# A linear-attention and SoLU kernel: the order of its work rewritten behind the first third, with halved squares and a new last unit

## The chip, the core and the metric

The kernel runs on one NeuronCore of a Trainium2 chip. The core has a matrix engine (TensorE: PE, with its weight loads listed apart as PEld), a vector engine (VectorE: DVE), an activation engine (ScalarE: ACT), a general engine (GpSimd: POOL) and a queue engine that mostly issues DMA transfers (SyncE: SP). Each has its own in-order queue, and they meet by semaphores. The metric is the device time of one execution in microseconds.

## What is computed

The first part is a linear attention with a decaying state, over 4 batches, 8 heads, 768 steps and head dimension 48. The second is a feed-forward layer on its output, read as 3072 tokens of 384 numbers: SoLU (h times softmax of h), a layer norm without shift, and the output product.

```python
for t in range(S):
    cur = einsum('bhd,bhe->bhde', u * k[t], v[t])
    y[t] = einsum('bhd,bhde->bhe', r[t], state + cur)
    state = w[t][..., None] * state + einsum('bhd,bhe->bhde', k[t], v[t])
h = x @ w_in                                   # 384 -> 1024
solu = h * softmax(h)
out = ((solu - mean) / sqrt(var + 1e-6) * g_ln) @ w_out   # 1024 -> 384
```

## The kernel before

The 768 steps are cut into six chunks of 128, and each chunk of each batch is a unit: unit i is chunk i // 4 of batch i % 4, 24 units in all. Inside a unit the recurrence is written as matrix products, and the state goes from unit i to unit i + 4.

One unit passes through these steps, each named by a word:

- LW, LK, LR, LV load the four inputs. The letter behind the point is the queue: none for SP, a for ACT, g for POOL.
- lw (ACT) takes the logarithm of the decays, cum (PE) sums it by two triangular matrices, ex (ACT) takes the exponentials in PSUM, and kp (DVE) multiplies keys and receptances by them.
- krk and krr (PE) turn these to the layout that the scores need and kr copies them from PSUM (ACT or DVE). In later units one DMA transpose, kt, takes the place of all three. It is issued by SP and reads and writes SBUF.
- M (PE) makes eight score blocks. m copies them out under the causal mask on DVE, or on ACT with the mask put on by POOL (sel).
- p, q (POOL), dg (DVE) and dv (POOL) make the diagonal term from r, k, u and v; vb casts v to bf16 on ACT or POOL.
- Y (PE) adds state and score products into y. Mode n leaves the diagonal term to y.d (DVE adds it while it copies y out); mode i adds it on PE by one more product of 384 columns with the identity, and then y.a copies on ACT.
- S (PE) makes the new state's sum, et (ACT) its decay, st (DVE) the decayed state. In mode n of S the old state is not added by PE: a DVE sum into the fp32 tile `sn_t` in SBUF goes ahead of the product. The old order uses this mode nowhere.
- X (three PE transposes) and xT (a copy) turn y for the next product; a DMA transpose on SP, xt, is the other way.
- H (24 matmuls of 128 columns) makes the hidden layer by columns, e (ACT) the exponential, he (DVE) their product, hq (ACT) the scaled square. For units named by an ht word the hidden layer is made by rows: six matmuls of 512 columns, and the statistics come from ACT's accumulators; a DMA transpose (ht) then turns he. The old order does this for units 16, 18 and 20.
- ea (POOL) adds the two halves of e, so that PE needs four sums of e in place of eight. The function `square_add` with its word qa does the same for the squares, in place; the old order has no qa word.
- Oa and Ob (PE) make the output's halves: per block of 128 hidden numbers one product of 386 columns and the sums over e and over the squares, one or two columns wide, in the same PSUM tile.
- qm (DVE), lv and rs (ACT) turn the sums into a scale, o scales the output (ACT or DVE) and out stores it from SP.

The last unit's hidden layer goes in halves (HA, HB, EA, EB, DA, DB, QA, QB). PSUM has eight banks, and the digit in a word says from which one it writes; a bank is free again when its last reader is done.

All this is written out by hand in one string, `ORDER`, of 881 words. The program runs through it and issues each word's instructions on its engine, so the string fixes the order on every queue. No planner moves anything afterwards. Rings of buffers bound how far a word may run ahead: 7 for inputs, 10 for lw and vb, 6 for kp, kr and dv, 4 for most others, 3 for p and q.

Almost every instruction is recorded under line 86 of the program, in the class `InOrder` that issues them, so the profile is read by tile names: `ps` is PSUM, `win_f` holds the row-wise he of the units named by ht, and `out<-in` names what is written and read.

Of the kernel before, what the change touches and what calls it, by code (L numbers as in the profile page):

```python
# [8 lines left out]
F32 = mybir.dt.float32  # L9
# [5 lines left out]
COPY = mybir.ActivationFunctionType.Copy  # L15
# [5 lines left out]
ORDER = """  # L21
# [11 lines left out]
Y5.n5 kp10 LR11 y5.d p8 LK11.a LK13 LW15 Ob1 X4.5 ex8 M7.1 lv0 krk10.4 rs0 kp8 q6 o0.a LK9.a vb6.p LW12 LR9 qm1  # L33
krr10 hq3.a dg6 cum11.6 q8 m7.d xT4.a Oa3.5 LV9.a lv1 out0 rs1 o1.a kr10.d out1 vb7.p vb8.a q7 ex11 LR12.g S7.0
LK12.a dv6 hq2.a LR14.g dg7 H4.2 et7 LK15.g lw9 e4 dg8 lw12 Ob3 kp11 st7 dv7 p10 krk8.1 qm3 cum9.6 Oa2.4 ex9 lv3
he4 Y7.n0 krr8 rs3 LW14.a o3.a Y6.n2 hq4.a kp9 y7.d LR17.g S6.3 Ob2 y6.d kr8.d p9 LW17 et6 X5.7 st6 LW19 qm2
LV12.a X7.2 krk11.6 vb9.a krr11 LR13 cum12.0 krk9.5 out3 xT7.d krr9 LK17 LK14 xT5.a lw15 lv2 kr11.d M8.2 q10 rs2
ex12 H5.6 o2.d q9 m8.a kp12 dv8 M11.3 lw13 S8.0 kr9.d m11.d p11 M9.1 LW16.a Oa4.5 e5 Ob4 m9.a et8 ea5.p he5
LR15.a X6.2 st8 vb11.p xT6.d sel8 out2 M10.3 p12 lw14 kt12 lw17 qm4 LV10 cum13.6 cum14.1 hot2.0 m10.d Y8.n0 S9.3
LR16.g hq5.a ex14 LW20 sel9 dg9 lv4 kp14 ex13 LW18.a Oa5.4 rs4 cum17.1 o4.a kp13 S11.5 y8.d et9 out4 cum15.6 Ob5  # L40
kt14 ex17 et11 ex15 Y9.n0 kp17 vb10.a H6.1 qm5 q11 dv9 lv5 rs5 LV15.g kp15 X8.6 st9 dg11 LR18.g y9.d LK16 o5.a
out5 lw19 dg10 e6 p13 kt15 H7.3 dv11 LV13 LW21.g xT8.a q12 he6 e7 vb12.p H8.6 hq6.a lw16 st11 he7 kt13 dg12
M12.1 X9.0 Oa6.5 p15 xT9.a dv10 Y11.n3 lw18 LK20.g m12.d Ob6 e8 p14 y11.d qm6 LV17 hq7.a he8 lv6 Y10.n2 LK18
M15.0 m15.d q13 rs6 y10.d dv12 q14 q15 H9.3 Oa7.7 Ob7 o6.a X10.0 LV14.a e9 LV16.g out6 hq8.a xT10.a he9 Y12.n5
p17 lw21 vb15.p vb14.p hq9.a xt11 qm7 y12.d M14.1 S10.3 Oa8.0 cum16.4 m14.d LK21.g et10 lv7 S12.1 st10 rs7
LK19.g LW22 dg15 dg13 Ob8 LR19.g vb13.a xt12 cum18.2 o7.a et12 ex16 H11.6 qm8 lv8 st12 kp16 out7 ex18 rs8 dv15
o8.a e11 dv13 S15.1 et15 dg14 H12.4 ea11.p e12 kp18 vb17.a q17 LR21 vb16.a out8 LV19.g LV21 lw22 he11 kt16
LV18.g hq11.a S13.3 p16 st15 Oa9.0 LR22.g Y15.n7 he12 LR20 y15.d Ob9 LK22 q16 M13.4 cum21.1 qm9 lv9 m13.d ex21
kp21 H10.6 p19 xt15 et13 rs9 Oa11.5 o9.a cum19.0 e10 Ob11 p18 st13 he10 qm11 hq12.a ex19 dg17 out9 Y13.n2 Oa12.4
Ob12 lv11 lw20 y13.d kt18 hq10.a rs11 dv14 vb19.p q18 M16.2 kt17 X13.7 kp19 Y14.n6 qm12 p21 vb18.a LK23 S16.0  # L50
xT13.a S14.7 lv12 rs12 o12.a m16.d y14.d cum20.1 et16 out12 et14 dg16 st14 q19 H13.3 H15.6 dg18 st16 ex20 xt14
o11.a Oa10.5 kp20 e13 dv16 M17.0 out11 ea13.p he13 dg19 cum22.2 e15 p20 ex22 dv17 Y16.i4 he15 Ob10 kp22 y16.a
H14.6 hq13.a e14 qm10 LW23.g q20 p22 M18.3 dv18 q22 ea15.p S18.2 LV20 lv10 kt19 m17.d Y17.n1 m18.d hq15.a Oa13.0
y17.d et18 dg20 st18 Ob13 rs10 he14 M19.3 ea14.p o10.a xt16 vb20.p qm13 H16.1 e16 kt22 dv20 Y18.n6 X17.5 m19.d
lv13 kt20 y18.d out10 xT17.a q21 rs13 Oa15.7 LV22.g Ob15 he16 M20.4 qm15 hq14.a S17.3 lv15 m20.d H17.1 dg21 et17
st17 kt21 M21.5 dv19 rs15 LR23 o15.a e17 m21.d Oa14.4 Ob14 he17 lw23 o13.a qm14 cum23.5 Y19.n3 xt18 Y20.n7 ex23
y19.d lv14 out15 y20.d ht16 LV23 ea17.p vb22.p rs14 vb21.a o14.a H18.0 p23 e18 X20.2 dg22 M22.3 S19.7 hq17.a
kp23 xT20.d m22.d Oa16.6 sv16 dv21 Y21.n5 hq16.a sv18 vb23.a Ob16 sq16 et19 H20.2 out13 he18 q23 y21.d dg23 dv22
e20 st19 xt19 he20 H19.0 Y22.n5 Oa17.7 kt23 e19 dv23 qm16 Ob17 y22.d ht18 M23.4 xt21 he19 lv16 rs16 o16.d Oa18.3
Ob18 hq20.a H21.0 hq18.a hq19.a m23.d ht20 xt22 out14 sq18 sv20 qm18 e21 lv18 ea19.p Y23.n2 rs18 Oa19.6 qm17  # L60
ea21.p lv17 rs17 y23.d Ob19 he21 Oa20.5 hq21.a qm19 out16 H22.0 o17.d xt23 lv19 o18.d rs19 Oa21.2 HA23.3 Ob21
out18 HB23.4 e22 Ob20 o19.d EA23 he22 hq22.a EB23 qm21 sq20 DA23 ea22.p lv21 qm20 lv20 DB23 QB23.d rs21 Oa22.7
# [38 lines left out]
def kernel(  # L101
# [14 lines left out]
    C = 128  # L116
# [462 lines left out]

    first_half, second_half = hidden_half(0), hidden_half(1)  # L580

    split = "out23.h" in ORDER.split()

    def output(i, part):
        L = live[i]
        e, he, hq, o_ps = e_t[i % NWK], he_t[i % NWK], hq_t[i % NWK], L["o_ps"]
        if i == NU - 1 and part and split:
            for f in range(KF // 2, KF):
                pe.matmul(o_ps[:, :DM + 2], lhsT=he[:, f, :], rhs=w2[:, f, :], start=False, stop=False,
                          skip_group_check=True)  # L590
            for f in range(KF // 2, KF):
                pe.matmul(o_ps[:, DM:DM + 2], lhsT=e[:, f, :], rhs=inv_col, start=False, stop=False,
                          skip_group_check=True)
            for f in range(KF // 2, KF):
                pe.matmul(o_ps[:, DM + 2:], lhsT=hq[:, f, :], rhs=one_col[:, :1], start=False, stop=(f == KF - 1),
                          skip_group_check=True)
            return
        for f in range(part * KF // 2, (part + 1) * KF // 2):
            if i in by_rows:
                pe.matmul(o_ps[:, :DM + 1], lhsT=he[:, f, :], rhs=w2[:, f, :DM + 1], start=(f == 0), stop=(f == KF - 1))  # L600
                continue
            pe.matmul(o_ps[:, :DM + 2], lhsT=he[:, f, :], rhs=w2[:, f, :], start=(f == 0), stop=False,
                      skip_group_check=True)
            if i not in added:
                pe.matmul(o_ps[:, DM:DM + 2], lhsT=e[:, f, :], rhs=inv_col, start=False, stop=False,
                          skip_group_check=True)
            elif f % 2 == 0:
                pe.matmul(o_ps[:, DM:DM + 2], lhsT=ea_t[i % NWK][:, f // 2, :], rhs=inv_col, start=False, stop=False,
                          skip_group_check=True)
# [37 lines left out]
    def scaled_out(i, x):  # L647
        o_ps, rs, o = live[i]["o_ps"], rs_t[i % NWK], o_t[i % NWK]
        if i == NU - 1 and split:
            act.activation(out=o[:, :DM // 2], in_=o_ps[:, :DM // 2], func=COPY, scale=rs)  # L650
            dve.tensor_scalar(out=o[:, DM // 2:], in0=o_ps[:, DM // 2:DM], scalar1=rs, scalar2=None, op0=MULT)
            return
        if x == "d":
            dve.tensor_scalar(out=o, in0=o_ps[:, :DM], scalar1=rs, scalar2=None, op0=MULT)
        else:
            act.activation(out=o, in_=o_ps[:, :DM], func=COPY, scale=rs)

    def store(i, x):
        c, b = units[i]
        rows = out[b * S + c * C:b * S + (c + 1) * C, :]  # L660
        if x == "h":
            act.dma_start(out=rows[:, :DM // 2], in_=o_t[i % NWK][:, :DM // 2])
            sp.dma_start(out=rows[:, DM // 2:], in_=o_t[i % NWK][:, DM // 2:])
            return
        queue[x].dma_start(out=rows, in_=o_t[i % NWK])

# [47 lines left out]
```

## Time and profile before

| | |
|---|---|
| time, median of 3 runs | 143.78 us (143.21 to 145.59) |
| the profiled execution's own time | 142.83 us |
| its span, first to last instruction | 141.0 us |
| PE busy | 125.5 us (89%) |
| DVE busy | 122.3 us (87%) |
| ACT busy | 118.9 us (84%) |
| POOL busy | 118.3 us (84%) |
| granted TensorE clock, mean | 0.99 |

The busy times are of one execution. Busy shares are averages over stages with different limits, so the stretches of the span have to be read apart. PE's matmuls are pipelined and their ends are modelled: a matmul's duration reaches beyond the start of the next one, and the time that one costs is the step from start to start.

### The profile page before, as it was taken

The page shows a single profiled execution, that of the slowest core. Times are in us where ns is not written, and L with a number is a line of the kernel's source. Part 1 is how long each engine was busy: PE and PEld are TensorE (multiplying, and loading weights), DVE is VectorE, ACT ScalarE, POOL GpSimd, SP SyncE. Part 2 cuts the span into 40 slices and gives each one's busy share as a digit, 9 for nine tenths or more (in the row PEclk, how much of TensorE's full clock was granted, in tenths as well). Part 3 has the DMA queues.
Part 4 walks back from the last instruction along what each step waited for, and adds up shares of the span by engine and source line. Part 5 has one row for each costly group of instructions (what it writes and reads, how often), then busy time and mean ns, then how long its engine had stood idle before and what let it go on. Part 6 is the DMA issues. An engine that isn't in the chain of part 4 may idle for free.

```text
span 141.0 us, 4797 instructions
## 1 busy us (share of the span) xinstructions
PE 125.5 (89%) x1890; PEld 94.6 (67%) x1890; DVE 122.3 (87%) x202; ACT 118.9 (84%) x243; POOL 118.3 (84%) x152
## 2 busy tenths in 40 slices
PE   0597956978999999999999999999999999999960
PEld 0136535657967887669877788788867766788740
DVE  6048879997999999999999998999999999878750
ACT  3648799979999999999989979998767889897780
POOL 7999999989999999999999999999999984402300
PEclk9999999999999999999999999999999999999996
DMA  4999999999999999999999999999999499652324
GB/s 89 274 298 343 323 278 388 382 307 232 263 234 237 285 297 295 242 227 223 297 190 238 188 242 213 291 224 162 186 228 213 97 255 86 144 170 78 123 73 154
DMA packets 94569, 31.98 MB, mean 227 GB/s; under 512 B 88569, under 2 KB 92674, under 8 KB 94546
## 3 DMA queue, kind: packets, MB, share of 16 engines
q1 hardware_dynamic: 70578, 20.92, 69.9%
q10 hardware_dynamic: 21984, 4.65, 15.6%
q0 software_dynamic: 1984, 6.10, 14.5%
q8 instruction: 15, 0.25, 0.8%
q14 instruction: 8, 0.07, 0.2%
HBM read 22.03 MB, written 4.72 MB: 190 GB/s over the span
## 4 chain that ended last, share of the span: by engine, by line
PE 40%; POOL 15%; DMA 13%; DVE 8%; ACT 5%; issue 2%; SPq 0%; ACTq 0%; POOLq 0%
PE ps L86 40%; DMA win_f<-in_moe_w_in_dram 5%; DMA kr_in<-in_k_dram 5%; DMA xT<-y 3%; POOL w L86 3%; POOL q L86 3%; DVE m L86 2%; POOL dv L86 2%; DVE he L86 2%; POOL m L86 2%; DVE y L86 1%; POOL win_sb L86 1%; ACT ps L86 1%; DVE kp L86 1%; POOL v_in L86 1%
## 5 line engine op out<-in xcount | busy, mean ns | idle before, releaser
L86 PE MATMUL ps<-w,he 128*128 128x386 bf16 (+1 forms) x192 | 43.2, 324 | 0.0
L86 PE MATMUL ps<-xT,win_sb 128*128 128x128 bf16 x504 | 31.2, 219 | 0.4 <-DMA xT<-y 0.2
L86 PEld LDWEIGHTS <-win_sb 128*128 128x128 bf16 x504 | 29.0, 98 | 2.1 <-DMA xT<-y 0.4
L86 ACT ACTIVATE e<-ps 128x1024 bf16<-128x1024 f32 (+1 forms) x25 | 24.6, 986 | 6.6 <-PE ps L86 5.0
L86 DVE TENSOR_TENSOR kp<-ps,kr_in 128x768 bf16<-128x768 f32 x24 | 22.7, 951 | 7.4 <-DMA kr_in<-in_r_dram 3.8
L86 PE MATMUL ps<-one_col,hq 128*128 128x1 bf16 x168 | 27.4, 163 | 0.0
L86 DVE TENSOR_TENSOR he<-ps,e 128x1024 bf16<-128x1024 f32 (+1 forms) x22 | 25.6, 1170 | 1.6 <-ACT e L86 1.3
L86 DVE TENSOR_TENSOR m<-ps,keep 128x1024 bf16<-128x1024 f32 x22 | 26.6, 1216 | 0.4 <-PE ps L86 0.4
L86 POOL TENSOR_TENSOR p<-kr_in 128x384 bf16<-128x384 f32 x24 | 24.0, 1004 | 0.3
L86 ACT ACTIVATE hq<-he 128x1024 bf16<-128x1024 bf16 (+1 forms) x21 | 21.6, 1030 | 0.7 <-DVE he L86 0.7
L86 POOL TENSOR_TENSOR q<-p,u_bc 128x384 bf16<-128x384 bf16 x24 | 21.7, 914 | 0.1
L86 POOL TENSOR_TENSOR dv<-vb,dg 128x384 bf16<-128x384 bf16 x24 | 19.8, 831 | 2.1 <-DVE dg L86 1.9
L86 ACT ACTIVATE ps<-ps 128x768 f32<-128x768 f32 x24 | 18.9, 796 | 2.6 <-PE ps L86 2.4
L86 PEld LDWEIGHTS <-he 128*128 128x128 bf16 x192 | 18.1, 96 | 3.5
L86 PEld LDWEIGHTS <-hq 128*128 128x128 bf16 x168 | 14.5, 96 | 8.8
L86 POOL TENSOR_TENSOR ea<-e 128x512 bf16<-128x512 bf16 x9 | 10.3, 1151 | 8.3 <-ACT e L86 8.3
L86 ACT ACTIVATE lw<-w_in 128x384 bf16<-128x384 f32 x24 | 12.3, 520 | 4.9 <-DMA w_in<-in_w_dram 4.9
L86 PE MATMUL ps<-inv_col,e 128*128 128x2 bf16 x96 | 15.8, 165 | 0.0
L86 PEld LDWEIGHTS <-kp 128*128 128x128 bf16 x176 | 11.8, 102 | 3.6 <-DVE kp L86 1.9
L86 PEld LDWEIGHTS <-kr 64*128 64x128 bf16 (+1 forms) x272 | 10.2, 95 | 5.3 <-issue 1.9
L86 DVE TENSOR_REDUCE dg<-q 128x8 f32<-128x384 bf16 x24 | 12.8, 544 | 0.2 <-POOL q L86 0.2
L86 DVE TENSOR_TENSOR st<-ps,et 128x384 bf16<-128x384 f32 x20 | 10.9, 549 | 0.6 <-ACT et L86 0.6
(97 smaller groups left out, 271.8 us busy)
## 6 DMA issues: line engine op xcount, KB each, us to landing
out_dram<-o SPq DMA_DIRECT2D x24, 192.0 KB, 3.7
kr_in<-in_k_dram SPq DMA_DIRECT2D x13, 192.0 KB, 5.8
kr_in<-in_r_dram POOLq DMA_DIRECT2D x12, 192.0 KB, 4.8
w_in<-in_w_dram SPq DMA_DIRECT2D x11, 192.0 KB, 5.2
kr_in<-in_r_dram SPq DMA_DIRECT2D x10, 192.0 KB, 4.8
v_in<-in_v_dram SPq DMA_DIRECT2D x10, 192.0 KB, 5.7
v_in<-in_v_dram POOLq DMA_DIRECT2D x9, 192.0 KB, 4.3
w_in<-in_w_dram ACTq DMA_DIRECT2D x8, 192.0 KB, 3.6
```

What stands on the lines that cost most here:

```text
L86: made = make(*args, **kwargs)
```

## The change

The first 250 words stay as they are. Behind them all words are in a new order, 633 of them in place of 631; queues, banks and modes change with them:

- x is turned by DMA in twelve units (8, 10, 11, 14, 15, 17 to 23) in place of ten (11, 12, 14, 15, 16, 18, 19, 21, 22, 23). Unit 14's keys and receptances are turned by PE, not by DMA.
- Unit 16 goes by columns like most others; only units 18 and 20 are left by rows.
- POOL halves the squares (qa) of units 12, 14, 15, 16, 17, 19 and 21, and the e of units 4, 7, 13, 16, 17, 19, 21 and 22 (before: 5, 11, 13, 14, 15, 17, 19, 21 and 22).
- S has mode n in units 12, 13, 14, 16 and 19. Y has mode i in units 8, 10, 11, 14 and 17 behind the cut, in place of unit 16.
- Two warm-up matmuls of 512 columns go. Several copies, casts and outputs change between ACT, DVE and POOL, and several loads change their queue: POOL issues one load more.
- The last unit's output has its first 256 columns in one bank, its sums of e and squares in a bank of their own, and the other 128 columns in a third. The sums are made ahead of most of the wide products. ACT scales and stores the 256 columns, DVE scales the 128 and SP stores them.

```diff
-    split = "out23.h" in ORDER.split()
+    ending = [word[2:].partition(".s") for word in ORDER.split() if word.startswith(f"Ob{NU - 1}.s")]
+    split = bool(ending)
+    DL = DM * 2 // 3
+
+    def last_output(i, part):
+        L = live[i]
+        e, he, hq = e_t[i % NWK], he_t[i % NWK], hq_t[i % NWK]
+        half = range(part * KF // 2, (part + 1) * KF // 2)
+        first = 2
+        if part == 0:
+            for f in range(first):
+                pe.matmul(L["o_ps"], lhsT=he[:, f, :], rhs=w2[:, f, :DL], start=(f == 0), stop=False)
+            L["s_ps"] = bank([C, 3], F32, ending[0][2][0], "s_ps")
+        s_ps = L["s_ps"]
+        for f in half:
+            pe.matmul(s_ps[:, :2], lhsT=he[:, f, :], rhs=w2[:, f, DM:], start=(f == 0), stop=False,
+                      skip_group_check=True)
+            pe.matmul(s_ps[:, :2], lhsT=e[:, f, :], rhs=inv_col, start=False, stop=False, skip_group_check=True)
+        for f in half:
+            pe.matmul(s_ps[:, 2:], lhsT=hq[:, f, :], rhs=one_col[:, :1], start=False, stop=(f == KF - 1),
+                      skip_group_check=True)
+        if part:
+            for f in range(first, KF):
+                pe.matmul(L["o_ps"], lhsT=he[:, f, :], rhs=w2[:, f, :DL], start=False, stop=(f == KF - 1))
+            r_ps = L["r_ps"] = bank([C, DM - DL], F32, ending[0][2][1], "r_ps")
+            for f in range(KF):
+                pe.matmul(r_ps, lhsT=he[:, f, :], rhs=w2[:, f, DL:DM], start=(f == 0), stop=(f == KF - 1))
...
-        o_ps = live[i]["o_ps"]
-        dve.tensor_scalar(out=qm_t[i % NWK], in0=o_ps[:, DM:DM + 1], scalar1=o_ps[:, DM + 1:DM + 2],
-                          scalar2=o_ps[:, DM + 2:], op0=MULT, op1=ADD)
+        s_ps = live[i]["s_ps"] if i == NU - 1 and split else live[i]["o_ps"][:, DM:]
+        dve.tensor_scalar(out=qm_t[i % NWK], in0=s_ps[:, :1], scalar1=s_ps[:, 1:2], scalar2=s_ps[:, 2:],
+                          op0=MULT, op1=ADD)
...
-            act.activation(out=o[:, :DM // 2], in_=o_ps[:, :DM // 2], func=COPY, scale=rs)
-            dve.tensor_scalar(out=o[:, DM // 2:], in0=o_ps[:, DM // 2:DM], scalar1=rs, scalar2=None, op0=MULT)
+            act.activation(out=o[:, :DL], in_=o_ps, func=COPY, scale=rs)
+            dve.tensor_scalar(out=o[:, DL:], in0=live[i]["r_ps"], scalar1=rs, scalar2=None, op0=MULT)
...
-QA23.a rs20 out17 Ob22 qm22 o20.a out19 lv22 Oa23.6 o21.d rs22 Ob23 out20 out21 o22.a qm23 lv23 rs23 out22 o23.a
-out23
+hq22.a lv20 rs20 EB23 DA23 Oa22.2 o20.d Ob22 QA23.a lv21 DB23 qm22 Oa23.0 QB23.d lv22 rs22 rs21 Ob23.s43 o22.a
+o21.a qm23 lv23 out20 rs23 out22 out21 o23.a out23.h
```

The last lines are the ends of the old and the new order.

More of the change, by code (lines that the diff above doesn't have):

```diff
@@ L37 @@
[L37 to L61, printed above, removed]
@@ new lines @@
+lv2 rs2 lw12 out0 LW16.a out1 LW14.g dv6 o2.a st6 S7.2 kr8.d et7 Ob3 LR17.g krk11.0 kp9 X5.1 M8.3 krr11 xT5.a
+st7 krk9.7 Y7.n2 m8.a qm3 dv7 lv3 out2 krr9 Y6.n6 kr11.d y7.d y6.d kr9.a M11.3 rs3 lw13 LK14 cum12.0 m11.d o3.d
+X7.2 ex12 kp12 ea4.p p9 H5.6 vb11.a e5 Oa4.5 xT7.d dv8 he5 M9.0 LR15.g M10.3 LK15 m10.d Ob4 LR16.g out3 lw14
+LW15.g qm4 m9.a cum13.6 LK17.a LV13 kt12 hq5.a q10 cum14.1 ex14 lv4 lw17 q9 sel8 LW19 S8.0 rs4 p12 X6.3 p11 et8
+LV12.a ex13 q11 o4.a dg9 xT6.d kp14 LV14.a sel9 dv9 st8 Oa5.4 kp13 Ob5 cum17.1 Y8.i3 lw15 ex17 dg11 S11.5 vb13.p
@@ new lines @@
+y8.a et11 q12 LK16 cum15.6 qm5 Y9.n0 S9.3 kp17 out4 ex15 st11 et9 kp15 lv5 H6.1 rs5 vb10.p dg10 st9 xt8 LW18.a
+o5.a e6 H7.4 y9.d dv10 e7 X9.0 dv11 krk14.3 Y10.i6 kt15 LV15.g LR19 krr14 ea7.p out5 xT9.a he6 Y11.i2 LV16.g
+LK18.a he7 y10.a lw16 kr14.d hq6.a y11.a M12.0 kt13 H8.6 m12.d H9.3 p13 S10.5 dg12 e8 M15.0 he8 e9 Oa6.2 m15.d
+vb12.a hq7.a Ob6 et10 M14.0 xt11 hq8.a he9 lw18 q13 p14 LW20.a vb15.a p16 S12.n6 LW21.g dg13 Oa7.7 dv12 Y12.n3
+LK19 Ob7 qm6 et12 lv6 LR18.g rs6 o6.a LK20 hq9.a m14.d y12.d qm7 S15.4 cum16.2 st12 ex16 lv7 q14 S13.n0 st10
@@ new lines @@
+LR21 Oa8.1 p15 rs7 o7.a q16 et15 LV19 Ob8 xt10 LR20 kp16 q15 dg14 vb14.a LK21.g et13 lw21 dv14 X12.5 qm8 xT12.a
+cum18.2 lv8 st15 ex18 H11.6 lw19 dg15 st13 p17 e11 vb16.p LV17.g kp18 rs8 H12.4 e12 out7 Oa9.0 he11 Ob9 p18 he12
+o8.a kt16 dv15 dg16 hq11.a qm9 cum21.1 ex21 kt17 LV18.g out6 Y15.n7 lv9 M13.3 q17 hq12.a y15.d q18 qa12.p H10.5
+kp21 e10 Oa11.7 cum19.1 Ob11 rs9 dv13 LW22.g ex19 m13.d lw20 he10 qm11 Y13.n4 vb18.p Y14.i3 o9.a hq10.a kp19
+out8 Oa12.6 lv11 vb17.a M16.1 y13.d xt15 kt18 LW23.g LV20 rs11 LK23 dg17 m16.d o11.a S14.n0 X13.5 et14 LK22.g
@@ new lines @@
+qm15 m20.d lv15 rs15 hq16.a Y20.n6 m21.d e17 o15.a out10 dv19 y20.d Ob14 he17 Y19.n3 cum23.5 y19.d p22 vb23.a
+vb21.a ea16.p qm14 LR23 qa16.p p23 ex23 S17.2 xt18 lv14 dg21 rs14 kt22 o14.a out15 kp23 xt20 q23 S19.n7 H18.0
+et17 et19 e18 M22.3 st17 xt19 Oa16.6 Y21.n2 out14 hq17.a ea17.p kt23 m22.d dv21 q22 he18 y21.d qa17.p dg23
+hq18.a ht18 dg22 Ob16 H20.4 e20 H19.0 st19 Oa17.7 vb22.p Y22.n2 qm16 Ob17 he20 e19 xt21 M23.3 dv23 Oa18.5 hq20.a
+lv16 rs16 out13 he19 Ob18 sv18 dv22 y22.d ea19.p hq19.a H21.1 qa19.p qm17 o16.a ht20 lv17 sv20 m23.d sq18 e21
@@ L586, in output @@
         e, he, hq, o_ps = e_t[i % NWK], he_t[i % NWK], hq_t[i % NWK], L["o_ps"]
[L587 to L596, printed above, removed]
+        if i == NU - 1 and split:
+            last_output(i, part)
             return
@@ L617, in output_a @@
     def output_a(i, x):
-        live[i]["o_ps"] = bank([C, DM + 3], F32, x, "o_ps")
+        live[i]["o_ps"] = bank([C, DL if i == NU - 1 and split else DM + 3], F32, x, "o_ps")
         output(i, 0)
@@ L661, in store @@
         if x == "h":
-            act.dma_start(out=rows[:, :DM // 2], in_=o_t[i % NWK][:, :DM // 2])
-            sp.dma_start(out=rows[:, DM // 2:], in_=o_t[i % NWK][:, DM // 2:])
+            act.dma_start(out=rows[:, :DL], in_=o_t[i % NWK][:, :DL])
+            sp.dma_start(out=rows[:, DL:], in_=o_t[i % NWK][:, DL:])
             return
```

15 lines of the change are left out of this document (10 added, 5 removed).

## The prediction

> **What bounds the kernel now.** I first read the page's busy line, then the table by stretches (columns: length; busy time and count of PE, its weight loads, DVE, ACT, POOL; granted clock; DMA share; GB/s), cut at 42.6 us, where the first rewritten word falls on PE.
>
> ```profile
> span 141.0 us, 4797 instructions
> PE 125.5 (89%) x1890; PEld 94.6 (67%) x1890; DVE 122.3 (87%) x202; ACT 118.9 (84%) x243; POOL 118.3 (84%) x152
> 42.60:72.00 29.40, 28.91 (x476) 22.81 (x473) 29.13 (x47) 28.25 (x57) 28.98 (x35) 1.00 1.17 265
> 72.00:82.00 10.00, 10.00 (x173) 8.07 (x172) 9.71 (x17) 8.97 (x21) 9.96 (x13) 1.00 1.17 200
> 82.00:112.00 30.00, 29.77 (x492) 23.33 (x490) 29.28 (x43) 24.82 (x51) 29.39 (x35) 1.00 1.11 204
> 112.00:136.40 24.40, 24.40 (x337) 17.81 (x335) 20.63 (x35) 21.14 (x51) 9.23 (x10) 1.00 0.58 134
> ```
>
> From 42.6 to 112 three engines are full together: PE, DVE and POOL. Behind 112 PE alone is full, and POOL works 9.2 of 24.4 us. Next I read the end of the chain that ended last (start, length, what).
>
> ```profile
> 82.33 54.11 PE ps L86 x822
> ...
> 136.47 0.30 DVE qm L86
> ...
> 136.79 0.21 ACT lv L86
> ...
> 137.26 0.58 ACT o L86
> ```
>
> So 54 us of matmuls without a wait set the end, then 1.4 us of the last unit's statistics and scaling. A busy PE needn't be PE at its peak, so I take its step from start to start in the order of time.
>
> ```profile
> 92.39 0.40 PE L86 MATMUL ps<-kr 64*128 64x128 bf16 x8
> ...
> 92.89 0.33 PE L86 MATMUL ps<-st,kr 128*128 128x96 bf16 x4
> 93.06 0.36 PE L86 MATMUL ps<-vb,m 128*128 128x48 bf16 x8
> 93.27 0.17 PE L86 MATMUL ps<-off_blocks,halves 128*128 128x8 bf16 x1
> ...
> 94.53 2.84 PE L86 MATMUL ps<-xT,win_sb 128*128 128x128 bf16 x48
> 97.21 0.33 PE L86 MATMUL ps<-w,he 128*128 128x386 bf16 x1
> 97.38 0.17 PE L86 MATMUL ps<-inv_col,e 128*128 128x2 bf16 x1
> 97.41 0.16 PE L86 MATMUL ps<-one_col,hq 128*128 128x1 bf16 x1
> 97.43 0.32 PE L86 MATMUL ps<-w,he 128*128 128x386 bf16 x1
> ...
> 118.32 0.81 PE L86 MATMUL ps<-win_sb,xT 128*128 128x512 bf16 x3
> 118.97 1.50 PE L86 MATMUL ps<-xT,win_sb 128*128 128x128 bf16 x24
> ...
> 120.69 0.32 PE L86 MATMUL ps<-w,he 128*128 128x386 bf16 x1
> ```
>
> The steps: 0.056 us for 128 columns ((97.21−94.53)/48), 0.163 for 384 or 386, 0.216 for 512 ((118.97−118.32)/3), and only 0.025 for a sum of one or two columns. Likewise 0.042 for 96 columns (93.06−92.89 for four), 0.026 for 48, and 0.4 for a unit's eight scores. The last row is unit 17's first output matmul. With these steps the words of the old order between the cut (42.50) and unit 23's first output matmul (at 134.57) add up to 90.0 us. PE therefore loses only 134.57−42.50−90.0 = 2.1 us to waits there. That and the end chain are all that an order can win; more must come from less work.
>
> **PE's own work.** Per matmul, up to unit 23's output: 128 columns 470 → 496 (+24 unit 16's hidden layer by columns again, +8 unit 14's keys and receptances back on PE, −6 two fewer x); 512 columns 20 → 12 (−6 unit 16, −2 warm-ups); 384 columns 43 → 42 (five states without the identity product, four more attends with it); sums 330 → 322 (six of the seven halved squares save four each, −24; one add of e less among the other units and unit 16 in columns, +16). Sum: 26·0.056 − 8·0.216 − 0.163 − 8·0.025 = **−0.6 us**. Halving a square saves PE 0.1 us. What it costs is in POOL's groups between 43 and 136 us (count | busy, mean ns | idle before):
>
> ```profile
> L86 POOL TENSOR_TENSOR q<-p,u_bc 128x384 bf16<-128x384 bf16 x18 | 16.3, 912 | 0.1
> L86 POOL TENSOR_TENSOR p<-kr_in 128x384 bf16<-128x384 f32 x16 | 16.0, 1004 | 0.3
> L86 POOL TENSOR_TENSOR dv<-vb,dg 128x384 bf16<-128x384 bf16 x18 | 14.9, 832 | 2.1 <-DVE dg L86 1.9
> L86 POOL TENSOR_TENSOR ea<-e 128x512 bf16<-128x512 bf16 x9 | 10.3, 1151 | 8.3 <-ACT e L86 8.3
> L86 POOL DMA_DIRECT2D kr_in<-in_r_dram x7 | 6.4, 911 | 0.3 <-POOL p L86 0.3
> L86 POOL CAST vb<-v_in 128x384 bf16<-128x384 f32 x9 | 4.4, 498 | 0.6 <-DMA v_in<-in_v_dram 0.6
> L86 POOL TENSOR_SCALAR_AFFINE_SELECT m<-m 128x1024 bf16<-128x1024 bf16 x2 | 2.2, 1092 | 0.0
> ...
> 43.07 0.90 POOL L86 TENSOR_TENSOR q<-p,u_bc 128x384 bf16<-128x384 bf16 x1
> 43.92 0.49 POOL L86 CAST vb<-v_in 128x384 bf16<-128x384 f32 x1
> ...
> 111.88 1.16 POOL L86 TENSOR_TENSOR ea<-e 128x512 bf16<-128x512 bf16 x1 [0.28 <-ACT e L86]
> ```
>
> **POOL, the term that decides.** No row shows the add of halved squares; the add of e has its shape and type, so I take 1.15 us, bounds 0.83 (the 384-column product) and 1.2. Seven cost 8 us. POOL's 11 idle us in these rows lie behind 111.88, where it first waits long, while five of the seven adds must be done for unit 17's output. Up to and with unit 17's halved square the new POOL queue holds 18 q, 15 p, 16 dv, 8 casts, 10 adds, 2 selects and 19 load issues (0.91 each). By the means that is 79.8 us. Neighbours overlap by 0.04 to 0.05 (the first two timed rows); 0.04 for the 69 pieces that aren't issues leaves 77.0. So it ends at 43.07 + 77.0 = 120.1 if POOL never waits, and at about 120.5 with half of the 0.9 us that POOL had idled by 111.88 in the old order. PE's work up to unit 17's output is 75.4 us, so PE could be there at 42.50 + 75.4 = 117.9. It must lose **2.6 us by then; it loses 2.1 now** (120.69 in the last PE row above, with 76.1 us of work behind the cut). The 13.9 us of PE work that are left put unit 23's output at 134.4, against 134.57: **−0.2**. A lower stall before unit 17 would win nothing, since POOL sets this end. With the bounds of the add it is −1.8 to 0.0; with no idle of POOL −0.6, with all of the 0.9 us +0.3.
>
> **DVE and ACT.** In the rows below (DVE and ACT groups of the whole span, then two DMA kinds with their median to landing, then the wait for a turned x): five states gain a sum into SBUF, which I price like the state product (0.549 each, +2.75; between the variance's 0.30 and the output's 0.61), while DVE gives up four y (−2.2), two outputs (−1.2) and a copy of x. DVE stays within 1 us. ACT gains seven pieces on balance (four y, two outputs, a copy of kr), none longer than the 1.02 us of that copy, and loses unit 16's accumulator reads and an x copy; it idles 5.2 of the 30 us from 82 to 112. I cost both at nothing; DVE's cover is thin, and 1 us too much on it would show in PE as 1 us.
>
> ```profile
> L86 DVE TENSOR_TENSOR st<-ps,et 128x384 bf16<-128x384 f32 x20 | 10.9, 549 | 0.6 <-ACT et L86 0.6
> L86 DVE TENSOR_TENSOR y<-ps,dv 128x384 bf16<-128x384 f32 x20 | 10.8, 549 | 0.3 <-issue 0.3
> L86 DVE TENSOR_SCALAR o<-ps,rs 128x384 f32<-128x384 f32 x6 | 3.6, 610 | 0.2 <-ACT rs L86 0.2
> L86 ACT COPY kr<-ps 128x1024 bf16<-128x1024 bf16 x4 | 4.1, 1017 | 0.2 <-PE ps L86 0.2
> kr<-kp SPq DMA_TRANSPOSE x12, 4.8
> xT<-y SPq DMA_TRANSPOSE x10, 3.7
>   DMA xT<-y: 0.2, 1
> ```
>
> **Transposes by DMA.** x goes 10 → 12, kr 12 → 11, he 3 → 2: SP still issues 25, so loads and stores queued behind them move little. A transpose lands in 3.7 us and PE waited 0.2 us once for one of x. The new early one, unit 8's, is issued about 64.5 and landed by 68.5 to 69.5, and PE, running some 1.5 us late there, comes for it at about 69.9. I cost these edits at nothing; if the cover goes, one late transpose costs 1 us.
>
> **The end.** Now unit 23's output starts at 134.57, and scaling ends 3.27 us later (137.26 + 0.58). In the new order PE has 0.5 us of the first half, then the sums, then 1.1 us of wide products (six of 256 columns at 0.11, eight of 128 at 0.056): the statistics no longer follow these. But DVE computes the second half's squares behind unit 22's variance, and ACT has unit 22's and 21's scalings ahead of unit 23's root. Along ACT, from the start of unit 23's output: unit 22's sums and variance 0.5, three small steps of units 22 and 21 at 0.23 (0.21 and a gap) 0.7, two outputs at 0.48 (the chain's 0.58, less 0.1 of overlap) 1.0, unit 23's two small steps 0.4, and its 256-column scaling 0.45 (between 0.21 for one column and 0.58 for 384): 3.0 us. **−0.3**, bounds −0.9 (both other outputs out of the way) and +0.3 (squares late, PE 0.4 longer). The store goes as two pieces on two queues instead of one, which no row shows: between 0 and −0.3, I take −0.1.
>
> Sum on the profiled execution's 142.83 us: −0.2 − 0.3 − 0.1 = −0.6, so 142.2. The median of the runs shown, 143.78, lies 0.95 above that execution; on their scale the forecast is **143.2 us**: no change by 2% (2.9 us, about what a measurement of this kernel tells from none).
>
> **Rivals.** *The waits add up* (chance 0.18). Before unit 9's attend the new POOL queue holds 6 q, 4 p, 3 dv, 2 casts, an add, 2 selects and 6 issues: 21.1 us, ending at 64.2. PE has 20.2 us of work and could be there at 62.7. These 1.5 us are swallowed by the 2.6 above unless the delay comes back to POOL through e, its squares or the diagonal sums that it waits for. For it: DVE is 99% busy in that stretch (29.13 of 29.40), so nothing catches up. Against: in the old order POOL idled only 0.9 us while PE lost 2.1. Time: 143.2 + 1.5 = 144.7.
>
> *Slower: two engines shut each other out* (0.14). In units 12, 13, 14, 16 and 19 DVE multiplies a state sum that lies in SBUF by a factor in SBUF; the large DVE products of the old order each read PSUM. If such a product and a POOL instruction excluded each other, POOL would lose 0.55 us each time and DVE up to a whole POOL piece, 1.0. Four lie ahead of unit 17's output: 4·0.55 = 2.2 if only POOL pays (145.4), 4·1.05 = 4.2 with half a piece of DVE's on the same chain (147.4); I take the middle, 146.4. From 0.15 us a time it makes the kernel slower than before. This is a rule of the Trainium skill (SBUF — State Buffer, "Who interferes with whom"): a Vector instruction with two SBUF inputs and a GpSimd instruction that reads SBUF take a shared port exclusively, and the later one blocks fully. No run here shows it.
>
> *POOL does not bind* (0.09): the adds of squares take 0.83, and PE's waits shrink to 1.0. Then 143.78 − 1.1 − 0.6 of work − 0.9 at the end = 141.2. For it: POOL's cover behind 112. Against: POOL is 98% busy from 82 to 112 already.
>
> *The change doesn't do what it says* (0.04): the x transposes of units 8 and 10 queue behind those of kr on SP and land late, so that PE gets less work but waits for them instead: two late by 1 us each, 145.2.
>
> The forecast itself, 142.2 to 144.2, has 0.55. Range: 141.4 to 146.8; it leaves out the outer half of the second rival, most of the third and what lies beyond the fourth. Faster by over 2% (below 140.9) only beyond the third: 0.05. Slower by over 2% (above 146.7): half of the second rival, a fifth of the first, half of the last, and chains of waits over several engines that these sums of single queues don't see: 0.16. Within: 0.79.
>
> **What would show it.** Right: unit 17's output waits for a POOL add and starts at 120 to 121 us; POOL is full up to there; behind it PE's share is 1.0; the last scaling ends 3.0 us after unit 23's first output matmul. The second rival: DVE or POOL pieces stretched by half a microsecond and more where the five states are multiplied. Wrong would be PE waits over 4 us behind the cut, a POOL that idles before unit 17, or an add of squares far from 1.15 us.

## The result: 4.6% slower, by DVE products that wait for GpSimd

The changed kernel takes 150.28 us in the median (149.17 to 152.05), beside 143.94 for the kernel before (six executions each): 1.046 times as long, with a 95% interval of 1.042 to 1.050. By this ratio that is 6.6 us more. Ratios here and below leave out slow executions, those over 1.5% above the fastest of their kernel: one of six on each side here, but six of ten in experiment 1, where the median of all ten is 1.009 of before's. The forecast was 143.2, in a range that ended at 146.8, so it was wrong; the mechanism was the second rival's, at over twice its price.

The profiled execution took 150.02 us. First its page, then the table by stretches (length; busy time and count of PE, its weight loads, DVE, ACT, POOL; granted clock; DMA share; GB/s).

```profile
span 148.3 us, 4848 instructions
PE 128.4 (87%) x1913; PEld 98.0 (66%) x1915; DVE 128.9 (87%) x201; ACT 121.4 (82%) x245; POOL 127.2 (86%) x159
```

```profile
42.60:72.00 29.40, 28.58 (x478) 23.29 (x475) 28.42 (x45) 27.42 (x56) 28.99 (x35) 1.00 1.19 251
72.00:82.00 10.00, 9.46 (x158) 7.11 (x156) 9.92 (x15) 9.43 (x22) 9.88 (x11) 1.00 1.23 214
82.00:112.00 30.00, 25.84 (x409) 21.16 (x408) 28.95 (x36) 22.99 (x45) 26.63 (x31) 0.94 1.02 186
112.00:136.40 24.40, 23.91 (x346) 17.42 (x344) 23.24 (x35) 19.66 (x42) 18.74 (x21) 1.00 0.63 119
```

The loss sits in the third stretch. PE was busy 29.77 of these 30 us; now it is busy 25.84, at a mean clock of 0.94. DVE alone is still full (28.95 of 30), while POOL has fallen from 29.39 to 26.63. An engine that stays full while the others thin out is the first to suspect. PE's own waits between 42 and 143 us say the same (what was waited for: us in total, times, longest), first of the changed kernel, then of the kernel before up to 135 us:

```profile
PE ps L86 <- DVE he L86: 2.9, 3, 2.3
PE ps L86 <- DVE kp L86: 1.8, 2, 1.3
PE ps L86 <- ACT lw L86: 0.4, 1, 0.4
PE ps L86 <- POOL m L86: 0.3, 1, 0.3
PE ps L86 <- DVE win_f L86: 0.3, 1, 0.3
PE ps L86 <- POOL hq L86: 0.2, 1, 0.2
```

```profile
PE ps L86 <- DVE m L86: 0.3, 1, 0.3
PE ps L86 <- DMA xT<-y: 0.2, 1, 0.2
PE ps L86 <- DVE kr L86: 0.2, 1, 0.2
```

The waits grew from 0.7 to 5.9 us, over the 4 us that the prediction named as a sign of being wrong. Of the 5.9 us, 5.0 end on DVE, and one wait is 2.3 us long. DVE's groups by operation and shape show what it does there (count | busy, mean ns | idle before):

```profile
L86 DVE TENSOR_TENSOR st<-sn,et 128x384 bf16<-128x384 f32 x5 | 9.0, 1805 | 0.2
L86 DVE TENSOR_TENSOR st<-ps,et 128x384 bf16<-128x384 f32 x15 | 8.1, 548 | 0.5 <-ACT et L86 0.4
L86 DVE TENSOR_TENSOR sn<-ps,st 128x384 f32<-128x384 f32 x5 | 2.7, 544 | 0.0
```

The same product of 384 columns takes 0.548 us when its first input is in PSUM and 1.805 us when it is in SBUF (`sn`): five of them cost DVE 6.3 us too much. The sums themselves take 0.544, close to the 0.549 that the prediction gave them. In the order of time (start, length, what) the two worst, units 14 and 16, look like this. DVE first:

```profile
96.46 2.37 DVE L86 TENSOR_TENSOR st<-sn,et 128x384 bf16<-128x384 f32 x1
98.75 0.94 DVE L86 TENSOR_TENSOR kp<-ps,kr_in 128x768 bf16<-128x768 f32 x1
99.62 0.54 DVE L86 TENSOR_TENSOR sn<-ps,st 128x384 f32<-128x384 f32 x1
100.20 2.84 DVE L86 TENSOR_TENSOR st<-sn,et 128x384 bf16<-128x384 f32 x1
102.96 1.21 DVE L86 TENSOR_TENSOR he<-ps,e 128x1024 bf16<-128x1024 f32 x1
...
96.78 1.62 POOL L86 TENSOR_TENSOR dv<-vb,dg 128x384 bf16<-128x384 bf16 x2
98.36 2.28 POOL L86 TENSOR_TENSOR p<-kr_in 128x384 bf16<-128x384 f32 x2
100.61 1.14 POOL L86 TENSOR_TENSOR ea<-e 128x512 bf16<-128x512 bf16 x1
101.72 0.90 POOL L86 TENSOR_TENSOR q<-p,u_bc 128x384 bf16<-128x384 bf16 x1
102.57 0.82 POOL L86 CAST vb<-v_in 128x384 bf16<-128x384 f32 x1
...
99.75 0.40 PE L86 MATMUL ps<-kr 64*128 64x128 bf16 x8 [1.26 <-DVE kp L86]
104.23 0.34 PE L86 MATMUL ps<-lw,uti_neg 128*128 128x384 bf16 x1 [2.26 <-DVE he L86]
```

DVE's first product ends at 98.83 and its second at 103.04, in both cases just after GpSimd goes from one piece to the next (98.36 and 102.57), and GpSimd's piece at that place is longer than usual (the cast 0.82 us; its mean before was 0.50). Behind each stand DVE words for which PE needs the bank: kp of unit 20 must have read the bank in which unit 17's scores are to be written, and he of unit 13 the one for unit 22's sums. PE waits 1.26 and 2.26 us.

### The profile page after: what moved, and what is told of

Read it like the earlier page. It is cut to its first block, busy times and chain, and to the rows that moved or that the text cites. A ratio compares the mean times of both kernels' runs of the same rounds, so it can differ in the third digit from the quotient of the medians.

```text
span 148.3 us, 4848 instructions
## 1 busy us (share of the span) xinstructions
PE 128.4 (87%) x1913; PEld 98.0 (66%) x1915; DVE 128.9 (87%) x201; ACT 121.4 (82%) x245; POOL 127.2 (86%) x159
## 4 chain that ended last, share of the span: by engine, by line
PE 43%; DVE 13%; ACT 9%; DMA 8%; POOL 7%; issue 4%; ACTq 0%; DVEq 0%
PE ps L86 43%; DMA w_in<-in_w_dram 4%; DVE st L86 3%; DMA out_dram<-o 3%; ACT hq L86 2%; DMA xT<-y 2%; DVE he L86 2%; POOL q L86 2%; DVE win_f L86 2%; POOL m L86 1%; ACT ps L86 1%; DVE sn L86 1%; DVE kp L86 1%; POOL p L86 1%; DVE dg L86 1%
## 5 line engine op out<-in xcount | busy, mean ns | idle before, releaser
L86 PE MATMUL ps<-w,he 128*128 128x386 bf16 (+4 forms) x208 | 43.8, 312 | 0.0
L86 PE MATMUL ps<-xT,win_sb 128*128 128x128 bf16 x528 | 33.5, 222 | 0.0
L86 PEld LDWEIGHTS <-win_sb 128*128 128x128 bf16 x528 | 31.5, 100 | 1.8
L86 DVE TENSOR_TENSOR he<-ps,e 128x1024 bf16<-128x1024 f32 (+1 forms) x23 | 26.7, 1170 | 2.6 <-ACT e L86 2.4
L86 ACT ACTIVATE hq<-he 128x1024 bf16<-128x1024 bf16 (+1 forms) x22 | 22.6, 1033 | 3.3 <-DVE he L86 3.3
L86 PE MATMUL ps<-one_col,hq 128*128 128x1 bf16 x148 | 23.4, 163 | 0.4 <-DVE hq L86 0.3
L86 PEld LDWEIGHTS <-hq 128*128 128x128 bf16 x148 | 13.0, 96 | 9.0 <-POOL hq L86 0.4
L86 PE MATMUL ps<-inv_col,e 128*128 128x2 bf16 x112 | 17.7, 164 | 0.0
L86 PE MATMUL ps<-lw,uti_neg 128*128 128x384 bf16 x23 | 8.0, 348 | 5.8 <-ACT lw L86 2.5
L86 PE MATMUL ps<-kr 64*128 64x128 bf16 x192 | 9.9, 218 | 2.6 <-DVE kp L86 1.3
```

The costliest lines, as they stand in the source:

```text
L86: made = make(*args, **kwargs)
```

## The experiments

**1. The five states back on PE.** The changed kernel with PE adding the old state by its identity product, so that DVE makes no sum.

```diff
-S12.n6 ... S13.n0 ... S14.n0 ... S16.n7 ... S19.n7
+S12.6 ... S13.0 ... S14.0 ... S16.7 ... S19.7
```

> The new kernel with the five states of units 12, 13, 14, 16 and 19 summed on PE again (one identity product of 384 columns each), all else as changed. Theory A, DVE's product of two SBUF tiles is held up by POOL: the five products of 1.2 to 2.8 us are gone, each state product takes 0.55 us, and the time falls by 5 to 8 us, to 142 to 145 us. Theory B, the new queue of POOL with its halved squares and the new order itself are what is slow: PE gets 0.8 us more work and the time stays at 148.5 to 151.

Measured: 0.997 times the time before (0.992 to 1.001). The whole loss is gone, so it is in these five words. A second comparison on another chip, beside experiment 9, gave 1.006 (1.002 to 1.010). The two intervals do not overlap, and the first ratio rests on four executions only. I take 1.001, the mean of the two, and count on at least half a per cent of doubt either way: that the loss of 4.6% is gone is clear, but a difference of less than one per cent between two kernels is not settled by these times.

> The kernel of the first experiment again, beside the one with the late states on DVE: on both theories 0.992 to 1.001 of before, as it was there. Were it over 1.003, the difference between the two would be less than the comparison can tell.

The 1.006 is over the 1.003 named there, so by this expectation the comparison in experiment 9 can tell little.

**2. The sum in PSUM.** The changed kernel with the same five sums on DVE, written to the bank that they read in place of the SBUF tile.

```diff
-            dve.tensor_add(out=sn_t[i % 2], in0=total, in1=st_t[b][(c - 1) % 2])
-            total = sn_t[i % 2]
+            dve.tensor_add(out=total, in0=total, in1=st_t[b][(c - 1) % 2])
```

> The new kernel with the same five states still summed by DVE, instruction for instruction, but the sum stays in PSUM, so that the product after it reads only one SBUF tile. Theory A (two SBUF inputs are what POOL holds up): the product takes 0.55 us as in the other units and the time falls to 142 to 145 us. Theory B (order and load, the product is only seen there): the product may get short, but the time stays above 148.

Measured: 1.009 (1.004 to 1.013). DVE makes just as many instructions as in the changed kernel (201); only the place where the sum is kept differs, and with it one input of the product. From its groups:

```profile
L86 DVE TENSOR_TENSOR st<-ps,et 128x384 bf16<-128x384 f32 x20 | 10.9, 553 | 1.6 <-ACT et L86 1.4
L86 DVE TENSOR_TENSOR ps<-ps,st 128x384 f32<-128x384 f32 x5 | 2.8, 557 | 0.0
```

All twenty products take 0.553 us again. That parts the loss in two: from 1.046 to 1.009, 3.7% or 5.3 us, is the product with both inputs in SBUF. The rest is the price of five more sums on DVE, with PE's five products saved, and its size is not settled: 1.2% or 1.7 us from 1.009 to experiment 1's 0.997 on the same chip, 0.8% to the 1.001 of both comparisons, and nothing to the 1.009 that all ten executions there give. The trace shows one way in which a sum costs: PE waits 0.41 us at unit 17's output, which is written to bank 7, until DVE has made unit 19's sum there and read it again for the product. Neither trace of experiment 1 has such a wait behind the cut.

**3 and 4. The same on the kernel before.** Its old order, with the five states on DVE: first with the sum in SBUF, then in PSUM (the edit of experiment 2 on top).

```diff
-S12.1 ... S13.3 ... S14.7 ... S16.0 ... S19.7
+S12.n1 ... S13.n3 ... S14.n7 ... S16.n0 ... S19.n7
```

> The kernel before with nothing changed but the five states of units 12, 13, 14, 16 and 19 summed by DVE into SBUF. Theory A: the products take 1.2 to 2.8 us also in the old order and the time rises by 3 to 8 us, to 147 to 152. Theory B: PE has 0.8 us less and DVE 2.8 us more work, so the time lies within 143 to 146.

> The kernel before with the same five states summed by DVE, the sum kept in PSUM. Theory A: products of 0.55 us and a time within 1.5 us of the kernel before (142.5 to 145.5), well below the run with the sum in SBUF. Theory B: the same time as that run.

Measured: 1.024 (1.014 to 1.034) and 1.011 (1.002 to 1.021), from three and four executions. The intervals overlap, so the times alone do not prove the sum in PSUM faster here. The products do show the hold-up, in the row of experiment 3:

```profile
L86 DVE TENSOR_TENSOR st<-sn,et 128x384 bf16<-128x384 f32 x5 | 4.2, 833 | 0.2
```

The hold-up needs neither the new order nor its squares on GpSimd: here the product takes 0.833 us. But the expected 1.2 to 2.8 us did not come: the five took 0.56 to 1.02 us. A likely reason, which was not tested, is that they meet GpSimd's pieces at other moments. The 1.1% of experiment 4 is near what the sums cost in experiment 2, but its trace does not tie it to them: PE's longest waits there, 1.7 us in two, are for a turned x.

**5. A probe of the product by itself.** DVE multiplies the same tile from SBUF ten times, with two products from PSUM between, beside GpSimd at rest (`alone`), at fp32 products (`product`), at casts (`cast`) and at adds (`add`); in `psum` DVE reads PSUM and GpSimd makes products.

> Not the kernel but the disputed cost by itself: all of the attention and the feed-forward layer is left out, and zeros are stored. DVE runs five stretches of ten times a 384-column product and two that read PSUM; POOL meanwhile is idle, then runs 384-column products of two SBUF inputs back to back (1.0 us each), the same beside a DVE product that reads PSUM and SBUF, casts of one input (0.5 us), and 512-column adds (1.15 us). If a two-input DVE product waits for POOL piece by piece: 0.55 us with POOL idle; with POOL's products 0.55 plus the rest of one piece, 0.8 to 1.6 us; with adds up to 1.7; with casts 0.55 to 1.1; the product from PSUM 0.55. If it can miss the gap between two pieces: some take 2 to 3 us, as in units 14 and 16. If POOL pays as well, its products grow from 1.0 to 1.2 us and more.

DVE's groups, then GpSimd's:

```profile
L37 DVE TENSOR_TENSOR dveproduct<-sn,et 128x384 bf16<-128x384 f32 x10 | 12.5, 1254 | 0.0
...
L37 DVE TENSOR_TENSOR dveadd<-sn,et 128x384 bf16<-128x384 f32 x10 | 6.2, 617 | 0.0
...
L37 DVE TENSOR_TENSOR dvealone<-sn,et 128x384 bf16<-128x384 f32 x10 | 5.5, 548 | 0.0
L37 DVE TENSOR_TENSOR dvepsum<-ps,et 128x384 bf16<-128x384 f32 x10 | 5.5, 547 | 0.0
```

```profile
L37 POOL TENSOR_TENSOR wideadd<-e 128x512 bf16<-128x512 bf16 x26 | 32.5, 1249 | 2.0
L37 POOL TENSOR_TENSOR poolproduct<-kr_in 128x384 bf16<-128x384 f32 x30 | 31.6, 1053 | 2.3
...
L37 POOL TENSOR_TENSOR poolpsum<-kr_in 128x384 bf16<-128x384 f32 x16 | 15.9, 995 | 1.2
```

Alone 0.548 us, beside GpSimd's products 1.254 (theirs then 1.053), from PSUM 0.547 with GpSimd untouched (0.995). Beside the adds DVE pays little (0.617) and GpSimd pays instead: 1.249 in the mean against 1.15 in the kernel before. It is the same beside casts: DVE 0.550, the casts 0.605 against 0.50. No product here took over 1.37 us, so none waited for more than one piece. That whoever comes second pays fits these rows; which one that is would then depend on how the two streams happen to meet.

**6. Five squares whole.** Experiment 1 without GpSimd's halving of the squares of units 12, 14, 15, 16 and 17, all that unit 17's output has to wait for.

```diff
-qa12.p ... qa15.p ... qa14.p ... qa16.p ... qa17.p
```

> The new kernel with the states summed on PE and without the halving of the squares of units 12, 14, 15, 16 and 17 (units 19 and 21 keep it). Theory A, POOL sets the time at unit 17's output as forecast: PE gets 0.5 us more work, POOL 5.75 us less, PE's waits behind the cut shrink by 1 us or more, and the time falls by 0.5 to 1.5 us against the run with the states on PE, to 0.985 to 0.995 of the kernel before. Theory B, PE reaches unit 17 no earlier than its square is halved anyway: the time rises by 0.3 to 0.8 us, to 0.997 to 1.003.

Measured: 1.005 (1.002 to 1.008), on a third chip, between the two results of experiment 1. Theory A, that GpSimd sets the start of unit 17's output, wanted 0.985 to 0.995; that did not come. Theory B's 0.997 to 1.003 was passed by a little. So 5.8 us less work for GpSimd brings no gain that these comparisons can tell; since experiment 1 is itself known to half a per cent only, a smaller one is not excluded by the time alone. The traces of experiment 1, read in the next section, say more.

**7. The new end alone**, on the kernel before: its last unit's output with the sums in their own bank and two stores.

```diff
-Ob23 ... out23
+Ob23.s43 ... out23.h
```

> The kernel before with the new last output alone (sums in a bank of their own and ahead of the wide products, 256 columns on ACT, 128 on DVE, two stores). By the forecast the last scaling ends 3.0 us after unit 23's first output matmul instead of 3.27 and the time falls by 0.4 us, to 0.997 (0.993 to 1.001). By the trace of the changed kernel, where it took 2.76 us, it falls by 0.5 to 0.7, to 0.995.

Measured: 1.001 (0.998 to 1.004): no gain. Its trace around the last unit, with the first output matmul, the two last scalings and SP's stores:

```profile
135.93 0.38 PE L86 MATMUL ps<-w,he 128*128 128x256 bf16 x3
...
136.69 2.43 SPq L86 DMA_DIRECT2D out_dram<-o  x4
...
137.98 0.47 ACT L86 ACTIVATE o<-ps,rs 128x256 f32<-128x256 f32 x1
138.11 0.35 DVE L86 TENSOR_SCALAR o<-ps,rs 128x128 f32<-128x128 f32 x1 [0.84 <-ACT rs L86]
```

The scaling ends 138.46 − 135.93 = 2.5 us after the first output matmul, 0.7 sooner than the old 3.3. But the span ends at 142.4, 3.9 us behind the scaling, where it was 3.2, so counted from the first output matmul it ends 6.4 to 6.5 us later in both kernels. SP issues its last four stores from 136.69 to 139.12, closely behind one another. The last unit's starts at 138.73, 0.27 us behind the scaling; in the kernel before it was 0.02 (137.86). So about a quarter of a microsecond is lost in SP's queue, and the rest behind the issue, in the transfers, perhaps behind those of the three stores just ahead. This is read from one trace; no run parts the stores.

**8. The two worst holds alone.** The changed kernel with only units 14 and 16 back on PE.

```diff
-S14.n0 ... S16.n7
+S14.0 ... S16.7
```

> The new kernel with only the states of units 14 and 16 summed on PE again; those of units 12, 13 and 19 stay in SBUF. In the changed kernel's trace the products of 14 and 16 took 2.37 and 2.84 us, 4.1 us beyond the usual, the other three 2.2 us beyond it. If the hold-up acts through those two waits of PE and the lower clock behind them: the time falls by 4 to 6 us, to 144.5 to 146.5. If every one of the five costs alike: it falls by two fifths of the loss, 2.5 us, to 147.5 to 148.5.

Measured: 1.012 (1.008 to 1.016), in the first range expected, so these two words, with their sums, make up 3.4%, 4.9 of the 6.6 us. The other three products still take more than twice their time:

```profile
L86 DVE TENSOR_TENSOR st<-sn,et 128x384 bf16<-128x384 f32 x3 | 3.9, 1297 | 0.1
```

Their 2.2 us of excess and three sums leave 1.2%. What a hold costs seems to depend on whether PE needs, just then, a bank that a DVE word behind it has to read: PE's waits for DVE, 5.0 us with all five, are 1.5 us here.

**9. Late states on DVE.** An attempt at a better version: experiment 1 with the states of units 17, 18 and 19 summed by DVE in PSUM, late, where DVE was 20.6 of 24.4 us busy in the kernel before.

```diff
-S18.1 ... S17.2 ... S19.7
+S18.n1 ... S17.n2 ... S19.n7
-            dve.tensor_add(out=sn_t[i % 2], in0=total, in1=st_t[b][(c - 1) % 2])
-            total = sn_t[i % 2]
+            dve.tensor_add(out=total, in0=total, in1=st_t[b][(c - 1) % 2])
```

> The kernel of the first experiment (all five states of units 12, 13, 14, 16 and 19 summed by PE), with the states of units 17, 18 and 19 summed by DVE in PSUM, in place of SBUF, behind 110 us where DVE has room. Saves PE three products of 0.163 us, adds three DVE sums of 0.55 us. Theory A (a DVE sum costs the end only where DVE is full, before 110 us): 0 to 0.5 us faster than the first experiment, so 142.7 to 143.3 us on the scale of before at 143.6, ratio to before 0.993 to 0.998. Theory B (a DVE sum in the chain from state to state costs its time wherever it lies): slower than the first experiment by 0.6 to 1.7 us, ratio 1.000 to 1.008.

Measured: 1.012 (1.008 to 1.017), beside experiment 1's 1.006 on the same chip: 0.9 us slower, with intervals that overlap a little. That speaks against Theory A, by which it had to be faster, without settling it; the ratio lies beyond Theory B's range too. The trace shows a cost that neither theory named: unit 17's output goes to bank 7, and that bank is free only when DVE has made unit 19's sum there (from 122.40) and read it again for the product (122.98 to 123.54). PE waits 0.77 us for it and goes on at 123.60. So a sum in PSUM can cost by the bank that it keeps, also where DVE has room; how much of the 0.9 us that is was not tested apart. No version that I ran beats the kernel before.

**10 and 11. Two probes of the long holds.** What stayed open was why units 14 and 16 held on for 2.4 and 2.8 us, which is more than any one GpSimd piece. The first probe ran one kind of GpSimd piece or a mixture; the second wrote the tile by a DVE sum just ahead of each product, and added load issues on GpSimd and squares on ACT.

> A measurement of the disputed cost by itself: the kernel's own work is left out and zeros are stored. In four stretches DVE multiplies a 128x384 fp32 tile in SBUF by a broadcast factor in SBUF twenty times, with one to five products from PSUM between them, while GpSimd runs one kind of piece or a mixture: fp32 products, bf16 products, bf16 products with a broadcast factor (the dv of the kernel), and a mixture of these with the add and the cast. Theory 1 (a DVE product with two SBUF inputs waits for the GpSimd piece that is running and gets in at its end): no DVE product of these takes more than its own 0.55 us and one piece, so 1.4 to 1.75 us at the most, in each stretch. Theory 2 (it can miss the gap between two pieces, as the products of units 14 and 16 appear to have done): some take 2 us and more, above all in the mixture; the means then lie over 1.1 us there. The products from PSUM stay at 0.55 us in both.

> What is still open is why the products of units 14 and 16 held on for 2.4 and 2.8 us, longer than any GpSimd piece. The kernel's own work is left out and zeros are stored. The tile in SBUF is now written by a DVE sum from PSUM right ahead of each product, as in the kernel, and GpSimd runs the mixture of its pieces, in the second stretch with the issue of an input load ahead of each round of them, in the third with scaled squares of 1024 columns on ACT beside it. Theory 1 (a waiting product gets in at the end of the piece that runs; something else held units 14 and 16): no product over 1.75 us in any stretch. Theory 2a (the issue of a load counts as a piece, or a product that arrives during one misses the next gap): over 2 us in the second and third stretch only. Theory 2b (traffic of ACT makes it miss the gap): over 2 us in the third only. Theory 2c (the write just ahead does): over 2 us in all three.

The mixture alone gave 0.546 to 1.392 us, with a median of 0.810. The stretch with all of it together (minimum, median, maximum in ns):

```profile
L37 DVE TENSOR_TENSOR dvebeside<-sn,et x20: 559/897/1398, 135.1 to 192.5; 128x384 bf16<-128x384 f32 x20
```

Theory 1 of both holds: in 140 such products none took over 1.41 us, one product and the rest of one piece. So in these probes neither the kind of piece, nor the sum ahead, nor a load issue, nor ACT makes a product miss the gap between two pieces. In the kernel the product of unit 14 waited across two pieces and that of unit 16 across three. What is different there (PE's reads, transposes by DMA, pieces that wait on other engines) wasn't tried apart, and the cause of the long holds stays open.

## Why the prediction was wrong

**The step that failed** is the price of the five states in the paragraph on DVE and ACT: the sum into SBUF was priced, "like the state product", at 0.549 us, and that was right (0.544); but the product behind it, which from then on reads `sn` in SBUF, was left at its old 0.549 and took 1.805. "DVE stays within 1 us" was therefore out by 6.3 us on the engine of which the same paragraph said that its cover is thin and that 1 us too much on it would show in PE as 1 us. It did, nearly: of the 6.6 us in the time, 5.3 are these products' (experiment 2). The rest of that reckoning held: DVE's busy time rose from 122.3 to 128.9 us, 0.3 more than the products account for.

**The second rival was right in kind, and priced too low.** It reckoned, for four times, 2.2 us if only GpSimd pays and 4.2 with half a GpSimd piece for DVE, and took the middle, 3.2. Measured: GpSimd paid about 1.2 us in all (its busy time is 127.2 us, and 126.0 in experiment 2 with the same 159 instructions), 0.24 for each product in place of 0.55, and DVE paid in all five, as the row of the tile says (minimum, median, maximum in ns):

```profile
L86 DVE TENSOR_TENSOR st<-sn,et x5: 1161/1349/2842, 79.2 to 127.2; 128x384 bf16<-128x384 f32 x5
```

The mean of 1.805 us is 1.26 beyond the undisturbed product, more than the "whole POOL piece, 1.0" that the prediction gave as the most, and with 0.6 the least that DVE paid is more than the half piece that went into the price. Its chance of 0.14 was low for a rule that the trace of before could not contradict, since no product there had two inputs in SBUF. The Trainium skill (SBUF — State Buffer, "Who interferes with whom") says that such a pair excludes each other whole, by order of issue, and that a DVE instruction with at most one SBUF input, outside the modes that use two ports, does not contend. Experiment 5 agrees with both (1.254 and 0.547 us); the holds of 2.37 and 2.84 us go beyond one blocking instruction, and there the measurement decides.

**GpSimd as the term that decides.** Two halves of this step parted. The sizes were right: the add of squares, which no row showed, was taken at 1.15 us and measures

```profile
L86 POOL TENSOR_TENSOR hq<-hq 128x512 bf16<-128x512 bf16 x7 | 8.1, 1151 | 4.2 <-ACT hq L86 3.9 <-ACT lv L86 0.3
```

and in experiment 1, where the hold-up is gone, the queue ends at 120.69, 0.2 us behind what the sum gave (120.1 to 120.5), and unit 17's output starts in the forecast 120 to 121:

```profile
119.55 1.14 POOL L86 TENSOR_TENSOR hq<-hq 128x512 bf16<-128x512 bf16 x1
119.56 1.50 PE L86 MATMUL ps<-xT,win_sb 128*128 128x128 bf16 x24
...
120.90 0.33 PE L86 MATMUL ps<-w,he 128*128 128x386 bf16 x1
```

But that GpSimd sets this end was not so. PE makes unit 19's hidden layer up to that moment without a wait, so the 120.90 in the forecast stretch is in part luck. In the second trace of experiment 1 the squares are there at 120.89 and the output starts at 121.72, 0.8 us later; in the changed kernel it is 125.67 and 127.22. Five adds less brought no gain either (experiment 6). A queue that ends at the same time as the work on PE need not be what holds PE.

**PE's own work**, −0.6, can't be read by itself; the 0.8 us that the five states save PE does not show as a gain in any run that has them, not even with the sum in PSUM (experiments 2 and 4). Without the five states the rest of the change comes to about 1.001 of before, 144 us on before's 143.78, where the whole was forecast at 143.2; half a per cent of doubt is 0.7 us, so this difference is not settled.

**The end.** In the changed kernel unit 23's first output matmul starts at 142.01 and the last scaling ends at 144.99:

```profile
142.01 0.38 PE L86 MATMUL ps<-w,he 128*128 128x256 bf16 x3
...
144.42 0.47 ACT L86 ACTIVATE o<-ps,rs 128x256 f32<-128x256 f32 x1
144.64 0.35 DVE L86 TENSOR_SCALAR o<-ps,rs 128x128 f32<-128x128 f32 x1 [0.90 <-PE ps L86]
```

The forecast 3.0 us came true, in part by luck. The sum went along ACT, whose scaling ends at 144.89, 2.9 us on; the last to end is DVE's, which waited for PE's last wide products (the 0.90 in its row). The 2.76 us in the expectation of experiment 7 do not agree with these rows. The store did not become shorter by 0.1: the span ends 3.3 us behind the scaling, before 3.2. So the end gives −0.1 and not −0.4, and alone nothing (experiment 7).

**The other rivals.** *The waits add up*: the first half came as feared. GpSimd's mask for unit 9 ended at 64.33 (forecast 64.2), and PE, which had begun that attend at 63.74, waited 0.32 us for it. But the delay did not run on: in experiment 1, where PE waited 0.55 us there, unit 17's output still starts at 120.90. *The change doesn't do what it says*: PE has no wait for a turned x in its list above. *POOL does not bind*: so it seems, but without the gain that the rival drew from it, since the time did not fall when GpSimd was relieved.

## What to carry to other kernels

Price an edit by the operands that its neighbours read afterwards, not only by the instructions it adds: here one tile in SBUF instead of PSUM made an unchanged product three times as long in one order and half as long again in the other. On an engine that is full, a DVE product that runs beside GpSimd should have an input in PSUM. Where it can't, its price here ran from nothing to 2.3 us beyond its own time, mostly the rest of a GpSimd piece, and all that stands behind it in DVE's queue waits as long. And a thin cover is a reason to look for everything that is added to that engine, not a reason to book it at nothing.

## What the runs showed that was not expected

A waiting product can lose more than one turn (2.37 and 2.84 us, above), but this was seen only in the changed kernel. GpSimd pays little there: its fp32 products measure 1.02 against 1.00 us and its casts 0.58 against 0.50.

PE's waits may cost more than their length. Two-microsecond stretches of the changed kernel (columns as above):

```profile
102.00:104.00 2.00, 0.00 (x0) 0.00 (x0) 2.00 (x2) 0.66 (x1) 2.00 (x3) 1.00 1.42 182
104.00:106.00 2.00, 1.77 (x22) 1.31 (x23) 2.00 (x3) 1.76 (x2) 1.23 (x2) 0.90 0.95 225
106.00:108.00 2.00, 2.00 (x29) 1.83 (x28) 2.00 (x5) 0.84 (x4) 0.00 (x0) 0.50 1.20 51
108.00:110.00 2.00, 2.00 (x29) 1.78 (x27) 1.05 (x3) 1.40 (x2) 1.49 (x2) 0.75 0.65 176
```

After the waits of 1.26 and 2.26 us the granted clock falls to 0.90, 0.50 and 0.75 for two microseconds each, which is 0.2 + 1.0 + 0.5 = 1.7 us of PE time. That is read from these rows and was not tested apart. Such a fall need not come from this change: the traces of experiments 1 and 2 show one near 24 us (0.50 from 24 to 26 us and from 24 to 30 us), in words that all these orders share, with no wait of PE over 0.9 us between 10 and 24 us. Executions of one kernel can differ by this too. The Trainium skill (TensorE: Matmul & The Clock Gate, "Part 1: The HAM clock gate") puts the fall to half speed behind an idle window of about 3.4 us; here no single wait is that long, but the two lie within six microseconds.
